# Retention and two expert blocks on one core: last Strassen product and two results of a pair moved among the next pair's, combinations on VectorE, loads two pairs ahead

## The chip, the cores and the metric

One NeuronCore of a Trainium2 chip runs the whole program. Its engines are TensorE (PE, whose weight loads are listed as PEld), VectorE (DVE), ScalarE (ACT), GpSimd (POOL) and SyncE (SP, which issues nearly all DMAs here). The metric is the device time of one execution in microseconds; lower is better.

## The reference, cut to what matters

```python
# q, k, v: (2, 8, 768, 64), lam: one decay per head
attn_out = retention(q, k, v, lam)           # decayed causal linear attention, state 64 x 64 per head
x = attn_out.transpose(0, 2, 1, 3).reshape(1536, 512)
h = x @ moe_w_in                             # 512 x 2048
x = (np.maximum(h, 0) ** 2) @ moe_w_out      # 2048 x 512
gate = 1 / (1 + np.exp(-(x @ moe2_w_gate)))  # 512 x 1536
return (gate * (x @ moe2_w_val)) @ moe2_w_out    # 1536 x 512
```

All of it is float32 on arrays of 1536 tokens. The kernel gets the weights as 64-bit numbers and turns them into float32 on the chip.

## The kernel before, in words

**Precision.** A float32 product is made from three single-pass products: each operand is split into a high half (a cast on ACT) and a low half (operand minus high half, a subtraction on DVE), and high x high, low x high and high x low are added in PSUM.

**Conversion.** The 68 weight units (128 x 512) arrive as raw 512 KB tiles, are converted by two ACT instructions (`conv_act`, L150, L151) and three DVE instructions (`conv_dve`, L172, L175, L167) and stored as 256 KB to a DRAM scratch `w32` (L169). Each `conv_act` issues the next raw load. `PACE` (L33) says how many conversions each step of phase 1 takes; `convert` (L752) places others on the agenda.

**Stages.** Tokens lie in three blocks of 512. Attention runs over 12 chunks of 128 tokens: seven ahead of the step loop, five inside it at the places of `SLOTS`. A chunk has `att_scores`, `att_prep` (on POOL `qd`, L279, and `kd`, L283; the decay mask on DVE, L289), `att_decay` (L298, POOL), `att_out` (L303: state product uv at L314, state part of the result at L323, the rest at L329), `att_state` (L336) and `att_x`. Block 0 of the tokens goes through phase 1 directly: 16 calls of `step_1`, each with 12 matmuls of `mm_in` (L393) and 12 of `mm_out` (L407). Blocks 1 and 2 together go through the input product of phase 1 by a Strassen scheme of seven block products per pair of weight units (`strassen`, L563; matmuls at L546), then through the output product (`pair_out`, L660). Phase 2 repeats this: 12 calls of `step_2`, 12 Strassen keys (gate and value for each of six pairs), `pair_out`. The last direct `stage_b` and its evacuation (`close`, L748) run inside the first Strassen pair of each phase.

**A Strassen key.** `load_a` (L506) reads two weight units as one 512 KB tile `a`. `combine_a` (L514) makes four sums and differences of its quarters into `as` on POOL (L518 to L521). `split_a` (L523) makes high halves (ACT, L527) and low halves (DVE, L528) of `a` and of `as`. The seven blocks are six matmuls each. Blocks A11, S2, S3 and A22 write bank x in that order, S1 and S4 bank z, A12 bank y. `snap` (L553, ACT) copies a bank aside; `total` (L558, DVE, L560) adds a bank and a copy. The four results go to `use`: in phase 1 a squared ReLU, in phase 2 a sigmoid (gate) or a product with the gate (value). `keep_g` (L586) stores each result (256 KB) to DRAM.

**x.** `combine_x` (L476) makes the seven x operands once per phase: differences T1 to T4 on POOL (L487), then high halves on ACT (L473) and low halves on DVE (L474).

**What sets the order.** The schedule is manual: each engine runs its instructions in the order in which the program issues them, and waits for data and for free buffers are added by the framework. A planner's clock advances by `MM` per matmul and by `SCORES` and `REST` per attention piece; `at(pos, fn)` puts work on an agenda, and `passed` runs what is due after each block of matmuls. T1 to T5 are the planned starts of the stages. Tiles come from pools of 27 tiles of 512 columns (`up`), 27 of 1024 (`wp`) and 8 PSUM banks.

```python
        block(x, key, S3, "T3", False, True)
        use(1, 1, total(x, s5), False)
        y = bank()
        block(y, key, A12, "B21", True, True)
        use(0, 0, total(y, s1), False)
        block(x, key, A22, "T4", False, True)
        use(1, 0, x, True)
```

These lines (L576 to L582) end a pair.

## Time and profile before

| what | value |
|---|---|
| median of 3 runs | 645.94 us (645.41 to 650.08) |
| the profiled execution | 650.61 us |
| its span, first to last instruction | 648.8 us |
| mean granted clock of PE, as a share of full speed | 0.968 |
| busy: PE, DVE, ACT, POOL | 604.2, 440.6, 333.1, 149.1 us |
| DMA | 127.18 MB, mean 196 GB/s |

A group is named by line, engine, operation and tiles; "idle before" is the time in which its engine had nothing running just before, and behind the arrow stands what ended that time. Matmuls are pipelined, so a group's mean exceeds the step from one matmul to the next. A stage's needs are read from that step, its losses from the waits of PE and the granted clock.

### The profile page before, as it was taken

How to read it: one execution, taken by the hardware profiler on the slowest of the kernel's cores; microseconds unless marked ns; L12 is line 12 of the kernel's file. 1: busy time of each engine (PE TensorE's matmuls, PEld its weight loads, DVE VectorE, ACT ScalarE, POOL GpSimd, SP SyncE). 2: the span in 40 equal slices, each digit the busy share in tenths (PEclk: the TensorE clock that was granted, in tenths of full speed). 3: DMA queues.
4: the chain of work that ended last, by engine and by line, in shares of the span. 5: the costliest groups of instructions: out<-in, count | busy, mean ns of one | idle time of the engine just before them, and what ended most of it. 6: DMA issues, size and time to landing. Idle time of an engine off the chain costs nothing.

```text
span 648.8 us, 8254 instructions
## 1 busy us (share of the span) xinstructions
PE 604.2 (93%) x2916; PEld 492.1 (76%) x2916; DVE 440.6 (68%) x595; ACT 333.1 (51%) x526; POOL 149.1 (23%) x122
## 2 busy tenths in 40 slices
PE   7889999995987888999999899999999999999997
PEld 6777888874765667888888688888877777778886
DVE  0799999967865566878866878776375546667201
ACT  0357788846454535756555466553544453456101
POOL 1671202129323150000003300044242345000000
PEclk9799999996988999999999799999999999999999
DMA  6967788680064437989996485540243133449003
GB/s 213 411 269 268 272 302 298 245 302 0 33 216 157 140 119 213 319 302 386 358 407 219 161 276 179 162 147 1 97 129 114 41 106 130 162 136 388 29 0 130
DMA packets 53434, 127.18 MB, mean 196 GB/s; under 512 B 5768, under 2 KB 7312, under 8 KB 53392
## 3 DMA queue, kind: packets, MB, share of 16 engines
q1 hardware_dynamic: 52376, 124.54, 54.5%
q10 hardware_dynamic: 1016, 2.11, 0.9%
q8 instruction: 23, 0.38, 0.2%
q14 instruction: 19, 0.16, 0.1%
HBM read 90.96 MB, written 35.66 MB: 195 GB/s over the span
## 4 chain that ended last, share of the span: by engine, by line
PE 72%; DVE 12%; DMA 6%; ACT 4%; issue 4%; POOL 1%; DVEq 0%; POOLq 0%; SPq 0%; ACTq 0%
PE p L660 23%; PE p L546 22%; PE p L393 14%; PE p L407 9%; DVE c L560 3%; DMA a<-w 2%; DVE al L528 2%; ACT ah L527 2%; DVE wlo L381 2%; PE p L329 1%; DMA D<-w_dram 1%; PE p L314 1%; DMA g<-g 1%; DVE m L175 1%; DVE m L172 1%
## 5 line engine op out<-in xcount | busy, mean ns | idle before, releaser
L546 PE MATMUL p<-xch,ah 128*128 128x512 f32 x280 | 113.1, 404 | 19.1 <-DVE c L560 18.4
L546 PE MATMUL p<-xcl,ah 128*128 128x512 f32 x280 | 110.8, 396 | 0.0
L546 PE MATMUL p<-xch,al 128*128 128x512 f32 x280 | 110.8, 396 | 0.0
L660 PE MATMUL p<-g2h,whi 128*128 128x512 f32 x224 | 87.1, 389 | 0.0
L660 PE MATMUL p<-g2l,whi 128*128 128x512 f32 x224 | 87.1, 389 | 0.0
L660 PE MATMUL p<-g2h,wlo 128*128 128x512 f32 x224 | 87.1, 389 | 0.0
L546 PEld LDWEIGHTS p<-xch,ah 128*128 128x128 f32 x280 | 53.6, 192 | 38.8 <-DVE c L560 26.2
L518 POOL TENSOR_TENSOR as<-a 128x512 f32<-128x512 f32 x20 | 29.1, 1457 | 205.0 <-DMA a<-w 78.8
L555 ACT COPY s<-p 128x512 f32<-128x512 f32 x60 | 35.2, 588 | 63.4 <-PE p L546 63.4
L546 PEld LDWEIGHTS p<-xch,al 128*128 128x128 f32 x280 | 53.5, 191 | 11.5
L546 PEld LDWEIGHTS p<-xcl,ah 128*128 128x128 f32 x280 | 53.6, 192 | 10.6
L528 DVE TENSOR_TENSOR al<-a,ah 128x1024 fp32r<-128x1024 f32 x20 | 27.7, 1384 | 46.3 <-ACT ah L527 44.7
L381 DVE TENSOR_TENSOR wlo<-u,whi 128x512 fp32r<-128x512 f32 x68 | 54.6, 831 | 2.2 <-ACT whi L379 0.8
L167 DVE CUSTOM_DVE_ANT_0 u<-m,r 128x1024 uint16<-128x1024 uint16 x68 | 53.5, 787 | 3.6 <-PE p L660 0.5
L175 DVE SCALAR_TENSOR_TENSOR m<-j,m 128x512 int32<-128x512 int32 x68 | 51.9, 763 | 1.3
L393 PE MATMUL p<-xh,wlo 128*128 128x512 f32 x160 | 44.8, 403 | 6.5 <-DVE wlo L381 6.5
L150 ACT ACTIVATE j<-raw 128x512 f32<-128x512 f32 x68 | 45.6, 671 | 8.6 <-PE p L407 3.4
L660 PEld LDWEIGHTS p<-g2l,whi 128*128 128x128 f32 x224 | 42.0, 188 | 8.8
L660 PEld LDWEIGHTS p<-g2h,whi 128*128 128x128 f32 x224 | 42.0, 188 | 8.7
L660 PEld LDWEIGHTS p<-g2h,wlo 128*128 128x128 f32 x224 | 42.0, 188 | 8.7
L151 ACT ACTIVATE r<-raw 128x512 int32<-128x512 uint32 x68 | 45.1, 663 | 6.4 <-PE p L660 4.9
L379 ACT CAST whi<-u 128x512 fp32r<-128x512 f32 x68 | 38.8, 617 | 14.7 <-DVE u L167 11.2
(86 smaller groups left out, 1045.9 us busy)
## 6 DMA issues: line engine op xcount, KB each, us to landing
raw<-in_w SPq DMA_DIRECT2D x68, 512.0 KB, 5.7
w<-u SPq DMA_DIRECT2D x68, 256.0 KB, 3.7
u<-w SPq DMA_DIRECT2D x64, 256.0 KB, 5.0
g<-g SPq DMA_DIRECT2D x56, 256.0 KB, 3.1
g<-g SPq DMA_DIRECT2D x28, 512.0 KB, 6.8
a<-w SPq DMA_DIRECT2D x20, 512.0 KB, 5.1
kv<-in_kv SPq DMA_DIRECT2D x12, 512.0 KB, 9.5
qk<-in_qk SPq DMA_DIRECT2D x10, 512.0 KB, 4.8
```

The source lines that it names most:

```text
L150: nc.scalar.activation(j, t[:, :, 1].bitcast(F32), AF.Copy, scale=2.0**-112)
L151: nc.scalar.activation(r, t[:, :, 0].bitcast(mybir.dt.uint32), AF.Copy, scale=2.0**-29)
L167: nc.vector.tensor_tensor(out=w.bitcast(I32), in0=m, in1=r, op=ALU.add)
L175: lambda: nc.vector.scalar_tensor_tensor(out=m, in0=j, scalar=-(2**31), in1=m, op0=ALU.bitwise_and, op1=ALU.bitwise_or),
L379: nc.scalar.copy(hi, src)
L381: lambda lo=lo, src=src, hi=hi: nc.vector.tensor_tensor(out=lo, in0=src, in1=hi, op=ALU.subtract)
L393: nc.tensor.matmul(acc, lhsT=a[:, kk * P : (kk + 1) * P], rhs=b[:, kk, :], start=i == 0, stop=i == 11,)
L407: nc.tensor.matmul(acc[e], lhsT=a[:, e * P : (e + 1) * P], rhs=b, start=first and i == 0, stop=last and i == 2,)
L528: nc.vector.tensor_tensor(out=lo, in0=src, in1=hi, op=ALU.subtract)
L546: nc.tensor.matmul(acc, lhsT=w[:, col, kk * P : (kk + 1) * P], rhs=x[:, kk, :], start=start and i == 0, stop=stop and i == 5, skip_group_c ...
L555: nc.scalar.copy(s, acc)
L660: nc.tensor.matmul(acc[e, t], lhsT=a[:, e * P : (e + 1) * P], rhs=b[:, t, :], start=first and i == 0, stop=last and i == 2,)
```

## The change

Within `strassen`, now one loop over all keys of a phase, block A22 and the results of A12 and A22 of a pair are issued inside the next pair: the sum for A12's result behind the next pair's A11 matmuls, A22 and its result behind the snap of the next pair's A11. `combine_a` and the differences of `combine_x` are issued on DVE instead of POOL. A key's load is issued at the start of the pair two ahead; high halves, combination and low halves for the next pair stand at fixed places in the pair. Results of a pair are stored together in the next pair. No conversions are placed in phase 1's products; 24 instead of 20 are placed in its output stage. PACE falls from 3 to 2 in steps 6 and 11, and to 1 and 0 in steps 14 and 15; as a step converts only while more than 36 units are left (`step_1`), step 13, which took none before, then takes two. Stores of converted weights fall due 4.0 instead of 1.0 planned us after conversion. In attention, uv and the state part are computed per head on tiles of 64, the state holds only the diagonal 64 x 64 blocks, `kd` is issued ahead of `qd`, and the state part comes after the rest. The weights of phase 2's first steps are loaded and split earlier. Agenda places and the planner's constants change accordingly.

```diff
-PACE = (2, 2, 2, 2, 2, 2, 3, 2, 2, 2, 2, 3, 2, 2, 2, 2)
+PACE = (2, 2, 2, 2, 2, 2, 2, 2, 2, 2, 2, 2, 2, 2, 1, 0)
...
-SCORES = 1.1
-REST = 3.3
+SCORES = 1.2
+REST = 2.6
...
-            at(clock[0] + 1.0, lambda: nc.sync.dma_start(out=w32[ph][f, u], in_=w))
+            at(clock[0] + 4.0, lambda: nc.sync.dma_start(out=w32[ph][f, u], in_=w))
...
-    S = [const.tile([P, 4, P], F32, name=f"S{i}", tag=f"S{i}") for i in range(2)]
+    S = [const.tile([P, 4, 64], F32, name=f"S{i}", tag=f"S{i}") for i in range(2)]
...
-        for st in S:
-            nc.vector.memset(st, 0.0)
...
-        if n > 0:
-            qd = qd_t[c] = unit("qd")
-            nc.gpsimd.tensor_tensor(out=pv(qd), in0=pv(qt), in1=L, op=ALU.mult)
...
+        if n > 0:
+            qd = qd_t[c] = unit("qd")
+            nc.gpsimd.tensor_tensor(out=pv(qd), in0=pv(qt), in1=L, op=ALU.mult)
...
-                out=pv(tt), in0=S[c // SEQ_CH],
-                in1=L[:, :, CH - 1 : CH].to_broadcast([P, 4, P]), op=ALU.mult,
+                out=pv(tt)[:, :, 0:64], in0=S[c // SEQ_CH],
+                in1=L[:, :, CH - 1 : CH].to_broadcast([P, 4, 64]), op=ALU.mult,
...
+        heads = [(p, r, slice(64 * r, 64 * r + 64)) for p in range(4) for r in range(2)]
...
         if n < SEQ_CH - 1:
-            kd = kd_t.pop(c)
-            uv = pv(bank())
-            for p in range(4):
+            kd = kd_t.pop(c).rearrange("s (h d) -> s h d", h=H)
+            uv = bank()[:, 0:256].rearrange("a (p e) -> a p e", p=4)
+            for p, r, b in heads:
                 nc.tensor.matmul(
-                    uv[:, p, :], lhsT=pv(kd)[:, p, :], rhs=pv(vt)[:, p, :], start=True, stop=True
+                    uv[b, p, :], lhsT=kd[:, 2 * p + r, :], rhs=v[:, 2 * p + r, :],
+                    start=p == 0, stop=p == 3, skip_group_check=True,
                 )
...
+        for p, r, b in heads:
+            nc.tensor.matmul(
+                ov[b, p, :], lhsT=v[:, 2 * p + r, :], rhs=pv(at[:, r, :])[:, p, :],
+                start=p == 0, stop=n == 0 and p == 3, skip_group_check=True,
+            )
...
-            qd = qd_t.pop(c)
...
+            qd = pv(qd_t.pop(c))
+            for p, r, b in heads:
                 nc.tensor.matmul(
-                    ov[:, p, :], lhsT=s[:, p, :], rhs=pv(qd)[:, p, :], start=p == 0, stop=False,
-                    skip_group_check=True,
-                )
...
-                    start=n == 0 and p == 0, stop=p == 3, skip_group_check=True,
+                    ov[b, p, :], lhsT=s[b, p, :], rhs=qd[b, p, :],
+                    start=False, stop=p == 3, skip_group_check=True,
...
-        ops = []
-        for r in range(2 if uv is not None else 0):
-            b = slice(64 * r, 64 * r + 64)
-            if tt is None:
-                ops.append(lambda b=b: nc.scalar.copy(s[b, :, b], uv[b, :, b]))
-            else:
-                ops.append(
-                    lambda b=b: nc.vector.tensor_tensor(
-                        out=s[b, :, b], in0=uv[b, :, b], in1=pv(tt)[b, :, b], op=ALU.add
-                    )
-                )
-        return ops
+        if uv is None:
+            return []
+        if tt is None:
+            return [lambda: nc.scalar.copy(s, uv)]
+        return [
+            lambda: nc.vector.tensor_tensor(out=s, in0=uv, in1=pv(tt)[:, :, 0:64], op=ALU.add)
+        ]
...
         nc.scalar.copy(hi, src)
-        nc.vector.tensor_tensor(out=lo, in0=src, in1=hi, op=ALU.subtract)
-
-    def combine_x(early, pos, gap):
-
+        at(
+            clock[0] + 1.3,
+            lambda: nc.vector.tensor_tensor(out=lo, in0=src, in1=hi, op=ALU.subtract),
+        )
...
-        at(early, lambda: split_x("B11", b11))
-        at(early + gap, lambda: split_x("B21", b21))
...
-            nc.gpsimd.tensor_tensor(
-                out=t[name], in0=t.get(a, a) if isinstance(a, str) else a,
-                in1=t[b] if isinstance(b, str) else b, op=ALU.subtract,
+            nc.vector.tensor_tensor(
+                out=t[name], in0=a, in1=t[b] if isinstance(b, str) else b, op=ALU.subtract
             )
...
             lambda: diff("T1", b12, b11),
             lambda: split_x("T1", t["T1"]),
             lambda: diff("T2", b22, "T1"),
             lambda: split_x("T2", t["T2"]),
+            lambda: split_x("B22", b22),
             lambda: diff("T3", b22, b12),
-            lambda: split_x("B22", b22),
             lambda: split_x("T3", t["T3"]),
             lambda: diff("T4", b21, "T2"),
             lambda: split_x("T4", t["T4"]),
...
-        tt = nc.gpsimd.tensor_tensor
+        tt = nc.vector.tensor_tensor
...
-    def split_a(key, part):
-        src = (a_t, as_t)[part].pop(key)
+    def high_a(key, part):
         hi = wp.tile([P, 4, 256], F32R, tag="w", name="ah")
         lo = wp.tile([P, 4, 256], F32R, tag="w", name="al")
-        nc.scalar.copy(hi, src)
+        nc.scalar.copy(hi, (a_t, as_t)[part][key])
+        s_t[(*key, part)] = hi, lo
+
+    def low_a(key, part):
+        hi, lo = s_t[(*key, part)]
+        src = (a_t, as_t)[part].pop(key)
         nc.vector.tensor_tensor(out=lo, in0=src, in1=hi, op=ALU.subtract)
-        s_t[(*key, part)] = hi, lo
 
     def prepare_a(key, pos):
 
-        at(pos - 22.0, lambda: load_a(key))
-        at(pos - 15.0, lambda: combine_a(key))
-        at(pos - 8.0, lambda: split_a(key, 0))
-        at(pos - 5.0, lambda: split_a(key, 1))
+        at(pos - 24.0, lambda: load_a(key))
+        at(pos - 14.0, lambda: combine_a(key))
+        at(pos - 12.0, lambda: high_a(key, 0))
+        at(pos - 9.0, lambda: low_a(key, 0))
+        at(pos - 8.0, lambda: high_a(key, 1))
+        at(pos - 5.0, lambda: low_a(key, 1))
...
-    def strassen(key, use, between=None):
...
+    def strassen(keys, uses, between):
+
+
+
+        after = between
+        for n, (key, use) in enumerate(zip(keys, uses, strict=True)):
+            nxt = keys[n + 1] if n + 1 < len(keys) else None
+            if n + 2 < len(keys):
+                load_a(keys[n + 2])
+            stores, held[:] = list(held), []
+            x = bank()
+            block(x, key, A11, "B11", True, True)
+            if n:
+                after[0]()
+            if nxt:
+                high_a(nxt, 0)
+                combine_a(nxt)
+            s1 = snap(x)
+            after[1]()
+            if nxt:
+                high_a(nxt, 1)
+            z = bank()
+            block(z, key, S1, "T1", True, True)
+            s5 = snap(z)
+            if nxt:
+                low_a(nxt, 0)
+            block(x, key, S2, "T2", False, True)
+            s2 = snap(x)
+            if nxt:
+                low_a(nxt, 1)
+            for fn in stores:
+                fn()
+            block(z, key, S4, "B22", False, True)
+            use(0, 1, total(z, s2), False)
+            block(x, key, S3, "T3", False, True)
+            use(1, 1, total(x, s5), False)
+            y = bank()
+            block(y, key, A12, "B21", True, True)
+
+            def first(use=use, y=y, s1=s1):
+                use(0, 0, total(y, s1), False)
+
+            def second(use=use, x=x, key=key):
+                block(x, key, A22, "T4", False, True)
+                use(1, 0, x, True)
+                for part in range(2):
+                    s_t.pop((*key, part))
+
+            after = first, second
+        after[0]()
+        after[1]()
+        for fn in held:
+            fn()
+        held.clear()
...
     def keep_g(ph, f, t, g):
-        at(clock[0] + 1.0, lambda: nc.sync.dma_start(out=g_dram[ph][f, :, t], in_=g))
-
-    def pair_in_1(i, between=None):
+        held.append(lambda: nc.sync.dma_start(out=g_dram[ph][f, :, t], in_=g))
...
-        combine_x(T1 - 40.0, T1 - 15.0, 1.6)
+        keys = [(1, i, 0) for i in range(NF1 // 2)]
+        prepare_a(keys[0], T1)
+        at(T1 - 20.0, lambda: load_a((1, 1, 0)))
+        combine_x([T1 + d for d in (-30, -25, -15, -13, -11, -9, -7, -4, -2, 1, 3)])
         for f in range(NF1):
             step_1(f)
-        n_in, n_out = 4, 20
-        for k in range(n_in):
-            convert(T1 + 10.0 + k * (T2 - T1 - 14.0) / n_in)
+        n_out = 24
...
+        uses = [use for i in range(NF1 // 2) for use in pair_in_1(i)]
+        strassen(keys, uses, (None, lambda: close(1)))
...
         for f in range(2):
-            at(T3 - 20.0 + f, lambda f=f: load_units(2, f))
-        at(T3 - 8.0, lambda: run(split_w(2, 0)))
...
-        for k in range(3 * NF2 - n_in - n_out):
+        for k in range(3 * NF2 - n_out):
...
+        keys = [(2, i, u) for i in range(NF2 // 2) for u in range(2)]
+        prepare_a(keys[0], T4)
+        at(T4 - 20.0, lambda: load_a((2, 0, 1)))
+        combine_x([T4 - 46.0 + 3.5 * k for k in range(11)])
```

## Rows read from the trace of the kernel before

**Rows 1.** The page, first part: busy us and share of the span.
```profile
PE 604.2 (93%) x2916; PEld 492.1 (76%) x2916; DVE 440.6 (68%) x595; ACT 333.1 (51%) x526; POOL 149.1 (23%) x122
```

**Rows 2.** Windows by stage: us; busy PE, PEld, DVE, ACT, POOL; clock; DMA; GB/s.
```profile
0.00:45.40 45.40, 36.88 (x364) 33.16 (x364) 25.98 (x44) 13.55 (x24) 23.46 (x23) 0.89 0.84 313
45.40:143.40 98.00, 96.39 (x559) 78.45 (x558) 93.54 (x149) 75.17 (x130) 17.51 (x12) 1.00 0.79 279
143.40:165.80 22.40, 13.96 (x42) 10.31 (x40) 16.52 (x10) 13.10 (x18) 19.40 (x12) 0.70 0.03 13
165.80:266.20 100.40, 85.74 (x350) 67.67 (x349) 64.66 (x82) 48.96 (x76) 26.24 (x24) 0.95 0.49 163
266.20:353.40 87.20, 87.20 (x386) 72.26 (x385) 66.55 (x98) 50.48 (x79) 1.89 (x1) 1.00 0.94 342
353.40:454.70 101.30, 98.17 (x421) 80.65 (x421) 80.13 (x103) 54.24 (x89) 23.50 (x16) 0.97 0.46 152
454.70:579.80 125.10, 120.61 (x517) 95.92 (x517) 69.36 (x85) 61.05 (x90) 37.13 (x36) 1.00 0.33 110
579.80:645.10 65.30, 65.26 (x288) 53.68 (x287) 23.16 (x28) 16.54 (x22) 0.00 (x0) 1.00 0.38 139
```

**Rows 3.** Waits of PE: who was waited for, us in total, times, longest.
```profile
PE p L546 <- DVE c L560: 18.4, 14, 3.8
PE p L407 <- ACT gh L434: 6.7, 1, 6.7
PE p L393 <- DVE wlo L381: 6.5, 4, 3.1
```

**Rows 4.** Window inside PE's longest wait in the step loop.
```profile
147.00:151.00 4.00, 0.00 (x0) 0.00 (x0) 1.72 (x1) 2.73 (x5) 3.92 (x3) 0.50 0.00 0
```

**Rows 5.** Timelines near 143 us: start, us, instruction, [idle before].
```profile
142.53 1.29 POOL L518 TENSOR_TENSOR as<-a 128x512 f32<-128x512 f32 x1 [16.83 <-DMA a<-w]
...
148.21 1.04 ACT L473 CAST xch<-t 128x1024 fp32r<-128x1024 f32 x1 [10.29 <-POOL t L487]
```

**Rows 6.** Timelines of DVE and POOL: the low half alone, and beside POOL.
```profile
213.06 1.23 DVE L528 TENSOR_TENSOR al<-a,ah 128x1024 fp32r<-128x1024 f32 x1 [2.80 <-ACT ah L527]
...
229.28 1.56 DVE L528 TENSOR_TENSOR al<-as,ah 128x1024 fp32r<-128x1024 f32 x1
...
229.72 1.70 POOL L521 TENSOR_TENSOR as<-a,as 128x256 f32<-128x256 f32 x1
```

**Rows 7.** Timelines of POOL and DVE at the start of phase 2's step loop.
```profile
354.23 2.46 POOL L487 TENSOR_TENSOR t<-xr,t 128x1024 f32<-128x1024 f32 x1 [0.31 <-POOL t L487]
...
354.47 2.77 DVE L175 SCALAR_TENSOR_TENSOR m<-j,m 128x512 int32<-128x512 int32 x1
```

**Rows 8.** Groups by line over the whole span: shape, count, busy us, mean ns.
```profile
L560 DVE TENSOR_TENSOR c<-p,s 128x512 f32<-128x512 f32 x60 | 39.6, 681 | 0.6 <-PE p L546 0.4
...
L555 ACT COPY s<-p 128x512 f32<-128x512 f32 x60 | 35.2, 588 | 63.4 <-PE p L546 63.4
...
L527 ACT CAST ah<-a 128x1024 fp32r<-128x1024 f32 x20 | 21.0, 1050 | 0.0
```

**Rows 9.** DMA issues of product weights; SP's longest wait.
```profile
a<-w SPq DMA_DIRECT2D x20, 512.0 KB, 5.1
...
SPq L509 <- DVE xcl L474: 25.0, 1, 25.0
```

**Rows 10.** Timeline of PE: the three matmul groups of one chunk's results.
```profile
113.31 1.05 PE L314 MATMUL p<-kv,kd 128*128 128x128 f32 x8
114.20 1.06 PE L323 MATMUL p<-qd,S 128*128 128x128 f32 x8
115.19 1.09 PE L329 MATMUL p<-at,kv 128*64 128x128 f32 x16
```

**Rows 11.** Windows of 10 us, output stage of phase 1.
```profile
270.00:280.00 10.00, 10.00 (x46) 8.26 (x45) 7.92 (x12) 5.45 (x9) 0.00 (x0) 1.00 1.01 348
...
330.00:340.00 10.00, 10.00 (x46) 8.29 (x45) 6.39 (x10) 5.14 (x8) 0.00 (x0) 1.00 1.04 408
```

More of the change, by code (lines that the diff above doesn't have):

```diff
@@ L336, in att_state @@
     def att_state(c):
-        n = c % SEQ_CH
         s = S[c // SEQ_CH]
@@ L502, in combine_x @@
         ]
-        for k, fn in enumerate(todo):
-            at(pos + k * gap, fn)
+        for pos, fn in zip(places, todo, strict=True):
+            at(pos, fn)
     def load_a(key):
@@ L561, in total @@
         return c
-    def strassen(key, use, between=None):
-        x, z = bank(), bank()
-        block(x, key, A11, "B11", True, True)
-        s1 = snap(x)
-        block(z, key, S1, "T1", True, True)
-        s5 = snap(z)
-        if between:
-            between()
-        block(x, key, S2, "T2", False, True)
-        s2 = snap(x)
-        block(z, key, S4, "B22", False, True)
-        use(0, 1, total(z, s2), False)
-        block(x, key, S3, "T3", False, True)
-        use(1, 1, total(x, s5), False)
-        y = bank()
-        block(y, key, A12, "B21", True, True)
-        use(0, 0, total(y, s1), False)
-        block(x, key, A22, "T4", False, True)
-        use(1, 0, x, True)
-        for part in range(2):
-            s_t.pop((*key, part))
+    def strassen(keys, uses, between):
[46 more added lines that the diff above has]
+        held.clear()
@@ L606, in use, with pair_in_2 @@
             keep_g(1, 2 * i + di, t, g)
-        strassen((1, i, 0), use, between)
-    def pair_in_2(i, between=None):
+        return [use]
+    def pair_in_2(i):
         gate = {}
@@ L805, in retention_moe_kernel @@
             prepare_out(1, f, T2 + 24 * MM * f)
-        for i in range(NF1 // 2):
-            pair_in_1(i, lambda: close(1) if i == 0 else None)
+        uses = [use for i in range(NF1 // 2) for use in pair_in_1(i)]
+        strassen(keys, uses, (None, lambda: close(1)))
         xc.clear()
@@ L827, in retention_moe_kernel @@
             prepare_out(2, f, T5 + 24 * MM * f)
-        for i in range(NF2 // 2):
-            pair_in_2(i, lambda: close(2) if i == 0 else None)
+        uses = [use for i in range(NF2 // 2) for use in pair_in_2(i)]
+        strassen(keys, uses, (None, lambda: close(2)))
         pair_out(2)
```

27 lines of the change are left out of this document (10 added, 17 removed).

## Prediction, before the change was run

> **What bounds the kernel now.** I read the page's first part, then the windows by stage, the waits of PE, the timelines around the long waits, and the groups by line.
>
> TensorE (PE) is busy for 93% of the span [rows 1]; the question is where the missing time lies. A 512-column matmul is issued every 0.2267 us where nothing waits: the output stage of phase 1 runs 384 of them in 87.05 us, and the windows put that stage at 87.2 us with PE always busy [rows 2]. Counting matmuls by that step gives what each stage would need (my stretches):
>
> - first steps up to 143.4 us: 98.0 us, PE idle 1.6;
> - end of the step loop, 143.4 to 165.8: 40 matmuls, 9.1 us; took 22.4: 13.3 lost;
> - Strassen products of phase 1: 8 keys of 42 plus 12, 78.9 us; took 100.4: 21.5 lost;
> - step loop of phase 2: 420, 95.2 us; took 101.3: 6.1 lost;
> - Strassen products of phase 2: 12 keys of 42 plus 12, 117.0 us; took 125.1: 8.1 lost;
> - both output stages: nothing lost.
>
> So 49 us are lost after the start, and they are waits, plus the slower clock that follows them. [rows 3] gives the kinds: 18.4 us of PE in 14 waits on `total` (L560), one of 6.7 us on a cast of ScalarE (ACT), 6.5 us on low halves of weights. After the wait of 6.7 us PE stood at a granted clock of 0.50 [rows 4], the lower of its two levels (1.2 of 2.4 GHz); the stage's mean was 0.70, that of phase 1's products 0.95 [rows 2], which alone is 5.0 of its 21.5 us.
>
> Causes. (a) In a pair the last block (A22) adds to bank x and must wait for the `total` that reads x; only block A12 (six matmuls, 1.36 us) lies between, and VectorE (DVE) does low halves and squares ahead of that `total`. (b) At 143 us GpSimd (POOL) starts the weight combination only when its load has landed, then does the x differences; ACT sits 10.3 us on the first of them, in front of the activations that PE needs [rows 5]. (c) Beside POOL, DVE's instructions on SBUF stretch: the same low half took 1.23 us alone and 1.56 beside POOL [rows 6]; at phase 2's start one instruction of a conversion took 2.77 us while POOL ran a difference [rows 7] that nobody needed for 50 us, and PE then waited 3.1 us for a low half [rows 3].
>
> **The change, part by part.** Sums are made against the profiled execution: 648.8 us of span and 1.8 around it, 650.6. That is 4.7 above the median of the runs, 645.9; I build the new time from counted work, take nothing off for it and let the lower end hold it.
>
> *Pipeline over pairs.* A22 of pair n-1 now comes after A11 of pair n, so two blocks (2.72 us) lie between S3 and A22. Is that enough? DVE's list per pair, by [rows 8]: three totals at 0.68, three squares at the same, two low halves at 1.23 [rows 6], and the combination, new on DVE: one of 512 columns (0.68) and three of 256. Those three are not in the trace on DVE; between half of 0.68 and 0.68 each, I take 0.42, nearest to half with a fixed part, 1.9 in all (1.7 to 2.7). Sum 8.4 us (8.2 to 9.2) of a pair's 9.52. DVE fits, in this order (0 is the start of A11): total and square 0.2 to 1.5, combination to 3.4, square of A22's result to 4.2, low halves to 6.6, total and square of z 7.0 to 8.3, total of x to 9.05. A22 is due at 10.88: 1.8 us of slack. ACT has two high halves at 1.05 and three snaps at 0.59 [rows 8] and in phase 1 three activations of a snap's width, 5.6 us. Its tight place is the snap of z: behind the second high half, which waits for the combination (3.5 to 4.5), it ends at 5.1, and S4 needs it at 5.44: 0.3 us. In phase 2 the value keys carry four products instead of three squares, 9.1 us: still under 9.52. So steady pairs should run without waits.
>
> The first pair carries more: the 12 matmuls of `close`, four casts and subtractions of `evacuate`, the last x terms; DVE some 12.6 us against 12.2. I leave 2.0 us lost in phase 1 (bounds 0, and 10 if half the present waits stay) and 0.8 in phase 2 (0 to 4). Gains: 21.5 - 2.0 = 19.5, and 8.1 - 0.8 = 7.3.
>
> *Loads two pairs ahead, stores grouped.* A load comes 9.5 us before its pair's turn and 11.0 before DVE wants it; they land in a median of 5.1 us [rows 9]. The load, then four grouped stores, share SP's queue; the stores' producers are done half a pair earlier, so SP waits for none. Cost nothing; uncovered, it is rival 4. The converted weights' stores, due 4.0 instead of 1.0 later, move no bytes. Buffers are tight: 14 x halves, 3 raw weights and the pairs' tiles make 27 of 27 when the combination is written, by my count; a wait for a free one would be on work already done.
>
> *Combinations on DVE at the end of the step loop.* Off goes wait (b), 13.3 us with its clock. In its place DVE gets, in the last 16.3 us, three x differences at 1.23 (a 1024-column instruction alone), the combination 1.9, five low halves 6.2, the steps' own four splits and three low halves 4.8, and two conversions that PACE moves here, at most three instructions of 0.68 each, 4.1: 20.7. That is over the room by 4.4 us; starts overlap, so I leave 3.0 lost (0.5 to 10). DVE is queued in order, so weight halves behind a difference are what PE would wait for. Gain 10.3.
>
> *Attention.* uv becomes 16 instructions of 64 moving columns for 8 of 128; the state part 16 of 64 rows for 8. Today these take 0.89 and 0.99 us from start to start, the 16 column-tiled ones of the third group 1.02 [rows 10]. uv: half of 1.02 at best, 1.02 at worst, I take 0.65, nearer to half as the columns halve; state part 0.5 to 1.02, I take 0.95, near today's 0.99. In the loop three chunks have the first and five the second: 3 x 0.24 + 5 x 0.04 = 0.9 us (-0.6 to +3.6). One state addition instead of two and half a decay on POOL also shorten the DVE and POOL queues; with `kd` ahead of `qd` the waits on L314 and the first low halves shrink: I estimate 2.0 us (0 to 4) over the seven chunks of the first 45.4 us, half an addition's 0.68 [rows 8] each, and 0.8 of the 1.6 idle in the loop. Gain 3.7.
>
> The Trainium skill, "TensorEngine Tiling (Array Packing)", section Instruction Overhead, speaks against the first of these: some 60 cycles are paid per matmul whatever its columns, and a small dimension should not be tiled again. By it uv would stay at the 1.02 us of its 16 instructions and this part would lose about 1 us; no row before shows 64 columns.
>
> *Output stage of phase 1.* Four conversions (768 KB each with the store: 3.15 MB in all) leave the products and come here, 24 for 20. The stage moved 342 GB/s at a DMA share of 0.94 [rows 2]: 29.8 MB; now 33.0. While the queues were full they moved 348 to 408 GB/s (the upper in [rows 11]), mean of six such stretches of 10 us, the first and last of which stand there, 378: 87.3 us for a stage of 87.05. Casts are placed 6.5 us ahead, and two casts and two low halves take some 3.5 [rows 6, 8], so a load may be 3 us late unseen. I take 1.0 us lost (0, as margin and unevenly used stretches absorb it, to 8.3, the extra bytes at 378).
>
> The Trainium skill, "SBUF — State Buffer", section Summary: rules for kernel authors, counts on about 358 GB/s between HBM and SBUF; 33.0 MB would then take 92.2 us, an estimate, 5 over the stage. [rows 11] shows 408 over 10 us, so I keep that for a rival.
>
> *Start of phase 2.* The weights' loads go 4 us and the first split 6 us earlier, and POOL's differences move to DVE 46 us before the products, after the conversions' stretch. DVE has 21 us free of 101.3 [rows 2]; four differences are 4.9. I leave 0.6 of 6.1 (0 to 3). Gain 5.5.
>
> Sum of gains: 19.5 + 7.3 + 10.3 + 3.7 - 1.0 + 5.5 = 45.3; 650.6 - 45.3 = **605.3 us**.
>
> **The rivals.**
> 1. *Output stage bound by DMA*: 8.3 instead of 1.0, 612.6 us. For: queues full at a share of 1.04 [rows 11]. Against: the stores no longer hold up SP, stretches at the stage's ends are free. By the figure that the Trainium skill gives above, 5 would stand for the 8.3.
> 2. *The end of the loop only changes its engine*: ACT's wait for POOL becomes PE's wait for DVE, 10 of 13.3 lost again: 612.3. For: DVE was busy 93.5 of 98 us there [rows 2].
> 3. *The pipeline does half of what it says*: `total` stays late behind combination and low halves: 10 and 4 lost in the products, +11.2: 616.5. For: 88% of DVE. Against: the slack of 1.8 us.
> 4. *Slower: a late load stops DVE.* The combination stands in DVE's queue behind the last `total` and before all that A22 needs. A load landing x us after its place delays A22 by x - 12.8 (11.0 and the slack), at 16 keys that are loaded so. Break-even with the gain of 45.3 is x = 15.6; at 16.5 it costs 59: 664 us. For: one load waited 25.0 us for a buffer in SP's queue [rows 9]. Against: median 5.1, and buffers are freed earlier now.
> 5. *Every cover holds*, and attention gains its upper bound: about 595.
>
> **How the numbers follow.** Forecast 0.58; rival 1 0.15, 2 0.10, 3 0.09, 4 0.04, 5 0.04. The forecast's own range is 600 to 610. To hold 8 in 10 I go from 597 (most covers) to 621 (rival 3 with some of another). About 1% is what a measurement of this kernel tells from no change: 639.5 and below is faster. Rivals 1 to 3, even two at once, stay below that, so faster 0.94, same 0.02 (several together), slower 0.04.
>
> **What would show it.** Right: no wait of PE on L560 over 1 us; granted clock 1.00 in both product stages; POOL empty after the last chunk; product stages near 81 and 118 us; the loop's end near 12; phase 2's loop near 96. Wrong steps: PE waits on weight low halves around 140 us (rival 2), gaps in the output stage with ACT waiting on DMA (rival 1), DVE waiting on `a<-w` (rival 4), the snap of z ending after S4's turn. The forecast is wrong if the product stages together lose over 12 us, or the time is outside 597 to 621.

## The result and the profile after

The changed kernel took 602.68 us (median of four runs, 601.90 to 603.98) where the kernel before took 646.45 (645.41 to 650.08): a ratio of 0.9316, interval 0.9275 to 0.9356. The forecast was 605.3 us in a range of 597 to 621. The profiled executions went from 650.61 to 602.85 us, their spans from 648.8 to 600.8.

The windows by stage of the changed kernel, in the columns of [rows 2], cut at the same places of the program (first steps, end of the step loop, products, output stage, and so on):

```profile
0.00:41.50 41.50, 32.61 (x460) 28.64 (x460) 23.40 (x39) 12.86 (x22) 21.73 (x23) 0.92 0.91 343
41.50:137.30 95.80, 95.36 (x622) 76.26 (x621) 90.36 (x148) 78.27 (x135) 14.74 (x11) 1.00 0.80 283
137.30:147.30 10.00, 9.34 (x41) 7.42 (x40) 9.96 (x14) 6.14 (x9) 0.00 (x0) 1.00 0.29 103
147.30:231.60 84.30, 80.67 (x349) 64.80 (x349) 68.58 (x100) 47.26 (x73) 0.00 (x0) 1.00 0.44 150
231.60:318.70 87.10, 87.10 (x386) 72.13 (x385) 73.63 (x110) 55.42 (x87) 0.00 (x0) 1.00 0.94 365
318.70:413.90 95.20, 95.20 (x422) 78.85 (x421) 74.81 (x112) 55.29 (x91) 0.00 (x0) 1.00 0.52 174
413.90:531.10 117.20, 117.20 (x517) 96.76 (x516) 85.15 (x129) 60.14 (x89) 0.00 (x0) 1.00 0.35 117
531.10:595.90 64.80, 64.80 (x287) 53.67 (x287) 23.11 (x27) 15.95 (x21) 0.00 (x0) 1.00 0.36 137
```

From 231.6 us on TensorE's busy time equals the length of every window, and the granted clock is 1.00 in all stages behind the first. The end of the step loop, 22.4 us at a clock of 0.70 before, takes 10.0 at 1.00. Most of what is still lost lies in the first 41.5 us and in one stage: the products of phase 1 take 84.3 us for 78.9 of work.

The waits of PE in the changed kernel, which answer to [rows 3]:

```profile
PE p L314 <- POOL kd L278: 3.6, 3, 1.9
PE p L264 <- DMA qk<-in_qk: 2.6, 2, 1.6
PE p L400 <- ACT gh L427: 2.4, 1, 2.4
...
PE p L386 <- DVE wlo L374: 1.0, 2, 0.7
...
PE p L545 <- DVE c L559: 0.6, 1, 0.6
PE p L545 <- ACT s L554: 0.6, 2, 0.3
```

The 18.4 us on `total` (now L559) have become 0.6, the 6.5 on low halves 1.0, the 6.7 on a cast 2.4. That last wait is the largest part of the 5.4 us that the products of phase 1 still lose. A timeline of the changed kernel around it, three engines in turn (start, us, instruction, idle before):

```profile
148.40 1.05 ACT L466 CAST xch<-t 128x1024 fp32r<-128x1024 f32 x1 [4.23 <-DVE t L480]
149.36 0.59 ACT L417 ACTIVATE r<-p 128x512 f32<-128x512 f32 x1
...
150.64 0.62 ACT L427 CAST gh<-g 128x512 fp32r<-128x512 f32 x1
...
147.15 1.22 DVE L480 TENSOR_TENSOR t<-xr 128x1024 f32<-128x1024 f32 x1
...
151.31 0.50 PE L400 MATMUL p<-gh,whi 128*128 128x512 f32 x1 [2.44 <-ACT gh L427]
```

It is the pattern of [rows 5] in small: ScalarE sits 4.23 us on the cast of a difference (T3) that VectorE starts only at 147.15, and the last activation of the step loop, which TensorE wants at once, stands behind it in ScalarE's queue.

### The profile page after: what moved, and what is told of

Read it like the earlier page. It is cut to its first block, busy times and chain, and to the rows that moved or that the text cites. A ratio compares the mean times of both kernels' runs of the same rounds, so it can differ in the third digit from the quotient of the medians.

```text
span 600.8 us, 8489 instructions
## 1 busy us (share of the span) xinstructions
PE 583.0 (97%) x3076; PEld 478.8 (80%) x3076; DVE 449.8 (75%) x673; ACT 331.9 (55%) x524; POOL 36.5 (6%) x34
## 4 chain that ended last, share of the span: by engine, by line
PE 84%; DVE 9%; DMA 3%; ACT 2%; issue 2%; POOL 0%; DVEq 0%; ACTq 0%; SPq 0%; POOLq 0%
PE p L545 30%; PE p L692 25%; PE p L386 16%; PE p L400 10%; DVE xcl L469 1%; PE p L322 1%; DMA D<-w_dram 1%; DVE m L175 1%; DVE wlo L374 1%; DVE u L167 1%; PE p L329 1%; DVE t L480 1%; PE p L264 1%; DMA lam_sb<-in_lam 1%; DVE at L287 1%
## 5 line engine op out<-in xcount | busy, mean ns | idle before, releaser
L545 PE MATMUL p<-xch,ah 128*128 128x512 f32 x280 | 109.6, 391 | 1.2 <-DVE c L559 0.6
L545 PE MATMUL p<-xcl,ah 128*128 128x512 f32 x280 | 109.0, 389 | 0.0
L545 PE MATMUL p<-xch,al 128*128 128x512 f32 x280 | 109.0, 389 | 0.0
L692 PE MATMUL p<-g2h,whi 128*128 128x512 f32 x224 | 87.1, 389 | 0.0
L692 PE MATMUL p<-g2l,whi 128*128 128x512 f32 x224 | 87.1, 389 | 0.0
L692 PE MATMUL p<-g2h,wlo 128*128 128x512 f32 x224 | 87.1, 389 | 0.0
L559 DVE TENSOR_TENSOR c<-p,s 128x512 f32<-128x512 f32 x60 | 41.2, 688 | 26.6 <-PE p L545 22.1
L545 PEld LDWEIGHTS p<-xcl,ah 128*128 128x128 f32 x280 | 52.6, 188 | 10.7
L167 DVE CUSTOM_DVE_ANT_0 u<-m,r 128x1024 uint16<-128x1024 uint16 x68 | 50.0, 736 | 2.7
L374 DVE TENSOR_TENSOR wlo<-u,whi 128x512 fp32r<-128x512 f32 x68 | 46.2, 708 | 7.0 <-ACT whi L372 5.7
L175 DVE SCALAR_TENSOR_TENSOR m<-j,m 128x512 int32<-128x512 int32 x68 | 49.5, 728 | 1.2
L372 ACT CAST whi<-u 128x512 fp32r<-128x512 f32 x68 | 39.1, 618 | 13.8 <-DVE u L167 13.3
L386 PE MATMUL p<-xh,wlo 128*128 128x512 f32 x160 | 43.2, 392 | 1.1 <-DVE wlo L374 1.0
L386 PE MATMUL p<-xh,whi 128*128 128x512 f32 x160 | 43.8, 395 | 0.0
```

Of the source, the lines that this page charges most:

```text
L167: nc.vector.tensor_tensor(out=w.bitcast(I32), in0=m, in1=r, op=ALU.add)
L175: lambda: nc.vector.scalar_tensor_tensor(out=m, in0=j, scalar=-(2**31), in1=m, op0=ALU.bitwise_and, op1=ALU.bitwise_or),
L372: nc.scalar.copy(hi, src)
L374: lambda lo=lo, src=src, hi=hi: nc.vector.tensor_tensor(out=lo, in0=src, in1=hi, op=ALU.subtract)
L386: nc.tensor.matmul(acc, lhsT=a[:, kk * P : (kk + 1) * P], rhs=b[:, kk, :], start=i == 0, stop=i == 11,)
L545: nc.tensor.matmul(acc, lhsT=w[:, col, kk * P : (kk + 1) * P], rhs=x[:, kk, :], start=start and i == 0, stop=stop and i == 5, skip_group_c ...
```

## The experiments

All twelve kernels compute everything. The first stage has the same code in ten kernels (the changed one and nine experiments made from it), and took 40.2 to 45.0 us there. In the three that took 44.6 to 45.0 (e1, e4, e10) the DMA queues moved 297 to 315 GB/s from 10 to 20 us and the granted clock from 20 to 30 us was 0.63 to 0.65; in the other seven it was 324 to 345 GB/s and 0.94 to 1.00. What starts this is not shown. So one execution can differ from another by up to 5 us for reasons that are no part of an edit, and I read the edits from the stages behind it. Each ratio is against the kernel before as it ran beside that experiment (medians 645.79 to 648.34 us). Stage lengths in us run from the first matmul of a stage to the first of the next, in the profiled execution:

| kernel | median us | ratio, interval | loop 1 | products 1 | output 1 | loop 2 | products 2 |
|---|---|---|---|---|---|---|---|
| before | 646.45 | | 120.4 | 100.4 | 87.2 | 101.3 | 125.1 |
| changed | 602.68 | 0.9316 [0.9275, 0.9356] | 105.8 | 84.3 | 87.1 | 95.2 | 117.2 |
| e1_own_pair | 612.01 | 0.9445 [0.9394, 0.9495] | 105.6 | 91.1 | 87.1 | 95.2 | 118.4 |
| e2_pool_a | 607.55 | 0.9391 [0.9331, 0.9450] | 108.1 | 86.4 | 87.1 | 95.7 | 117.2 |
| e3_pool_x | 606.37 | 0.9357 [0.9312, 0.9402] | 112.9 | 79.4 | 87.1 | 97.2 | 117.3 |
| e4_conv_in | 606.19 | 0.9364 [0.9315, 0.9414] | 105.7 | 88.3 | 87.0 | 95.2 | 117.2 |
| e5_before_dve | 632.89 | 0.9767 [0.9738, 0.9796] | 111.4 | 99.6 | 87.1 | 95.2 | 124.7 |
| e6_before_places | 630.63 | 0.9738 [0.9708, 0.9769] | 121.6 | 88.5 | 87.0 | 100.3 | 117.3 |
| e7_late_half | 602.80 | 0.9307 [0.9281, 0.9333] | 106.2 | 83.9 | 87.1 | 95.2 | 117.3 |
| e8_late_own | 617.60 | 0.9537 [0.9510, 0.9564] | 105.8 | 91.7 | 87.0 | 95.2 | 124.6 |
| e9_t3_late | 600.71 | 0.9290 [0.9259, 0.9320] | 105.8 | 81.3 | 87.0 | 95.2 | 117.3 |
| e10_conv30 | 608.09 | 0.9410 [0.9373, 0.9446] | 105.4 | 84.3 | 92.5 | 95.2 | 117.3 |
| e11_load_late | 601.46 | 0.9311 [0.9275, 0.9348] | 105.9 | 83.9 | 87.1 | 95.2 | 117.3 |
| e12_dve_places | 615.42 | 0.9530 [0.9486, 0.9575] | 112.6 | 89.0 | 87.0 | 95.2 | 117.6 |

### The pipeline over pairs

**Undone in the changed kernel.** The results of A12 and A22, and the block A22, go back to the end of their own pair.

```diff
-            if n:
-                after[0]()
...
-            after[1]()
+            if n == 0:
+                between[1]()
...
-            after = first, second
-        after[0]()
-        after[1]()
+            first()
+            second()
```

> The changed kernel, with block A22 and the results of A12 and A22 issued again at the end of their own pair; everything else as changed (combinations on VectorE, loads two ahead, no conversions in the products). Theory A, the place of A22 is what removed the waits on `total`: one block of 1.36 us lies again between S3 and A22, so PE waits for L559 in most of the 20 pairs, some 0.5 to 1.0 us each with the restart, 10 to 18 us in all: 613 to 621 us. Theory B, the waits came from what stood ahead of `total` in VectorE's queue (stretched low halves, conversions), and those are gone: by the order worked out for a pair, the total of x ends 0.4 us before A22 is due even at the old place, so the time stays within 3 us: 602 to 606 us.

612.01 us, between the two theories. The products of phase 1 lose 6.8 us more than in the changed kernel, those of phase 2 only 1.2, where the kernel before lost 8.1. The waits of PE in this kernel; its timeline in a steady pair of phase 1 (ACT, PE) and in a value key of phase 2 (DVE):

```profile
PE p L545 <- ACT s L554: 2.8, 6, 0.5
...
PE p L545 <- DVE c L559: 1.9, 1, 1.9
```

```profile
183.46 1.05 ACT L520 CAST ah<-as 128x1024 fp32r<-128x1024 f32 x1 [0.94 <-DVE as L515]
184.42 1.06 ACT L554 COPY s<-p 128x512 f32<-128x512 f32 x2
...
185.05 0.50 PE L545 MATMUL p<-xch,ah 128*128 128x512 f32 x1 [0.50 <-ACT s L554]
...
458.70 1.22 DVE L526 TENSOR_TENSOR al<-as,ah 128x1024 fp32r<-128x1024 f32 x1 [0.21 <-ACT ah L520]
461.21 0.69 DVE L559 TENSOR_TENSOR c<-p,s 128x512 f32<-128x512 f32 x1 [1.28 <-PE p L545]
```

Without the pipeline TensorE of phase 1 waits for a snap in every steady pair: the combination comes late on VectorE, behind the totals of the pair before, ScalarE waits 0.94 us for it, and the snap of z stands behind. That is the place that the prediction called tight (0.3 us of room). The rest of the 6.8 us comes mostly from the one wait of 1.9 us on `total`, in the first pair, and from the clock behind it, by this window of e1:

```profile
167.20:171.20 4.00, 3.97 (x10) 3.20 (x11) 1.66 (x3) 2.29 (x4) 0.00 (x0) 0.57 0.51 197
```

In the value key nothing on TensorE waits for `total`: VectorE has the second low half done and is idle 1.28 us before the next total. So something else had removed the wait on `total` in phase 2. In `split_a`'s agenda the second low half came behind block S4; the change also moved it ahead, right behind the first.

**The second low half back behind S4, with the pipeline (e7) and without it (e8).**

```diff
-            if nxt:
-                high_a(nxt, 1)
...
-            if nxt:
-                low_a(nxt, 1)
...
             block(z, key, S4, "B22", False, True)
+            if nxt:
+                high_a(nxt, 1)
+                low_a(nxt, 1)
```

> The changed kernel, with the second high and low half of the next pair put directly ahead of the total of z, where they stood before; A22 stays in the next pair. Theory C with two covers: the total of x then ends about 10.5 us after the start of the pair's A11; A22 is due at 10.9, so it still fits: phase 2's products stay within 2 us of 117.3, phase 1's within 4 of 84.3, 602 to 608 us. If the place of the halves alone decides, products lose 0.7 to 1 us per key: 616 to 623 us.

> Both undone in the changed kernel: second halves directly ahead of the total of z, and A22 with the two results in their own pair. Theory C with two covers: neither undone alone costs much in phase 2, both together do; the total of x ends about 10.5 us after the start of A11 and A22 is due at 9.5: about 1 us and the restart per key, phase 2's products 127 to 132 us, phase 1's 95 to 100: 625 to 640 us. Theory B, the totals were only late because of GpSimd and conversions, which are gone here: as with A22 alone in its own pair, 610 to 615 us.

e8 is this edit and e1's together. e7 is the changed kernel within 0.2 us; e8 takes 617.60 us, less than the 625 to 640 of its theory C, and has most of phase 2's loss back, 124.6 us. Its waits of PE, and its timeline in a value key (ACT, DVE, PE):

```profile
PE p L545 <- DVE c L559: 10.0, 12, 1.7
```

```profile
458.31 1.05 ACT L520 CAST ah<-as 128x1024 fp32r<-128x1024 f32 x1
...
459.39 1.23 DVE L526 TENSOR_TENSOR al<-as,ah 128x1024 fp32r<-128x1024 f32 x1 [2.93 <-ACT ah L520]
460.53 0.68 DVE L559 TENSOR_TENSOR c<-p,s 128x512 f32<-128x512 f32 x1
461.25 0.69 DVE L648 TENSOR_TENSOR g<-c,r 128x512 f32<-128x512 f32 x1
461.86 0.68 DVE L559 TENSOR_TENSOR c<-p,s 128x512 f32<-128x512 f32 x1
...
462.60 0.50 PE L545 MATMUL p<-xch,ah 128*128 128x512 f32 x1 [0.79 <-DVE c L559]
```

VectorE idles 2.93 us for a high half whose cast is issued late, behind the snap of S2 on ScalarE, then does the low half in front of two totals and a product, and A22 is 0.79 us late. Each of the two edits is enough in phase 2 (e1 loses 1.2 us there, e7 0.1); only without both does the loss come back.

**The places alone, in the kernel before.**

```diff
-        at(pos - 8.0, lambda: split_a(key, 0))
-        at(pos - 5.0, lambda: split_a(key, 1))
+        at(pos - 9.0, lambda: split_a(key, 0))
+        at(pos - 7.0, lambda: split_a(key, 1))
```

> The kernel before, with one thing changed: the two splits of the next pair's weights stand at 9 and 7 planned us ahead instead of 8 and 5, which puts the second high and low half behind block S1 instead of behind S4. Theory C, the products lost time because the second low half, waiting for its high half on ScalarE, stood in VectorE's queue directly ahead of the totals: phase 2's products go from 125.1 to 117 to 120 us, phase 1's (with conversions and GpSimd as before) from 100.4 to 86 to 95: 627 to 637 us. Theory A, it is the place of A22, one block behind S3: products within 3 us of before, 642 to 648 us.

Two numbers in the kernel before, and it takes 630.63 us, as theory C had it: the products of phase 2 go to 117.3, those of phase 1 from 100.4 to 88.5. The wait on `total` of 18.4 us in 14 [rows 3] is now, among PE's waits,

```profile
PE p L546 <- DVE c L560: 4.9, 3, 2.2
```

### The combinations on VectorE

**Weight combinations back on POOL (e2), x differences back on POOL (e3)**, each in the changed kernel:

```diff
     def combine_a(key):
...
-        tt = nc.vector.tensor_tensor
+        tt = nc.gpsimd.tensor_tensor
```

> The changed kernel with the weight combination (four instructions per key) on GpSimd again; the pipeline and everything else stay. Theory A, the engine matters by its speed and by what it does to VectorE beside it: the four take about 4.5 us there instead of 1.9, the second high half and with it the snap of z come 2 to 3 us late, low halves stretch from 1.23 to 1.5 us and more: PE waits on L554 about 1.5 to 2.5 us per pair, 25 to 45 us in all: 628 to 648 us. Theory B, the pipeline alone hides the combination wherever it runs: within 4 us of the changed kernel, 602 to 607 us.

```diff
         def diff(name, a, b):
...
-            nc.vector.tensor_tensor(
+            nc.gpsimd.tensor_tensor(
```

> The changed kernel with the differences T1 to T4 of x on GpSimd again. Theory A, they caused the loss at the end of the step loop and at the start of phase 2: ScalarE sits again on the first difference, VectorE is stretched beside GpSimd; 5 to 12 us come back at the end of the loop. In phase 2 they now stand late on the agenda, but GpSimd is free and starts when the data are there, so 2 to 5 us come back at its start: 609 to 619 us. Theory B, the late load of the first combination caused it (it is issued two planned us earlier now): at most 3 us come back, 602 to 606 us.

e2: 607.55 us, near theory B. 2.3 us more in the loop, 2.1 in the products of phase 1, nothing in phase 2's products. Steady pairs don't lose by the engine that combines, though low halves beside POOL take up to 1.88 us in e2; the first combination does. PE's wait on `gh` grows:

```profile
PE p L400 <- ACT gh L427: 5.1, 2, 4.3
```

e3: 606.37 us, between the two theories. The loop takes 7.1 us more, phase 2's loop 2.0, the products of phase 1 4.9 less, as the differences run early on POOL and leave VectorE free by then. The price is a late low half of weights in the loop:

```profile
PE p L386 <- DVE wlo L374: 7.5, 4, 5.7
```

It is late because VectorE's weight combination now runs beside the differences on POOL. One instruction of each in e3, and the same VectorE instruction in the changed kernel:

```profile
131.86 2.74 POOL L480 TENSOR_TENSOR t<-xr,t 128x1024 f32<-128x1024 f32 x1
132.25 2.63 DVE L513 TENSOR_TENSOR as<-a 128x256 f32<-128x256 f32 x1
```

```profile
132.51 0.42 DVE L513 TENSOR_TENSOR as<-a 128x256 f32<-128x256 f32 x1
```

The four instructions of that combination take 2.91, 2.63, 2.59 and 2.56 us, 10.7 in all instead of 1.9; the low half stands behind them. ScalarE waits only 0.4 us for a difference in this stretch, so what comes back in e3 is not wait (b) of the prediction but the stretching of (c).

**Both on VectorE, in the kernel before (e5), and that with e6's two numbers (e12).** e5 is e2's and e3's line in the other direction; e12 is e5 and e6 together.

> The kernel before, with the weight combinations and the x differences on VectorE, at the places where it had them; no pipeline, conversions stay in the products. Theory A, GpSimd cost the most at the end of the step loop and at the start of phase 2: these two stages get shorter by about 8 and 5 us. In the products the combination then stands in VectorE's queue ahead of the totals of its pair (15 planned us before the next pair): 0 to 1 us more per key, 0 to 20 us. In all 633 to 650 us. Theory B, the engine is the main cause in the products too: all stages shorten, 620 to 630 us.

> The kernel before with two small edits together, each tried alone already (x differences and weight combinations on VectorE: ratio 0.977; the second low half directly behind the first in ScalarE's and VectorE's order: 0.974). If they act on different waits, as the stages say (the end of the loop and phase 2's loop by the one, the products by the other), they add: ratio 0.945 to 0.955, 611 to 617 us, with phase 2's products at 117 to 118 us, its loop at 95 to 96, and the first loop near 111. Rival (the vector engine with both becomes the bound of the products, and the pipeline over pairs is what makes room for the combination there): products of phase 1 stay near 99 and the ratio near 0.97.

e5: 632.89 us. The loop is 9.0 us shorter, phase 2's loop 6.1 and at its 95.2 us of work; the products keep their losses. Its wait on `total`:

```profile
PE p L546 <- DVE c L560: 16.9, 12, 3.8
```

e12: 615.42 us, where the sum of the two single gains (15.1 and 16.9 us against a kernel before of about 646) gives 614. The two act on different waits and add. Windows of e12 for the products of phase 1 and of phase 2, in the columns of [rows 2]:

```profile
155.50:244.50 89.00, 82.28 (x350) 64.16 (x349) 73.19 (x110) 50.70 (x80) 0.00 (x0) 1.00 0.54 178
...
426.70:544.30 117.60, 117.60 (x517) 96.50 (x516) 83.34 (x125) 60.68 (x90) 0.00 (x0) 1.00 0.35 117
```

So some 30 of the 44 us come from an engine's name in two places and two numbers in an agenda; the rest of the change, the pipeline, the attention and the placing of conversions among it, brings the other 13.

### Conversions and the output stage

**Four conversions back among the products (e4); six more in the output stage (e10).**

```diff
-        n_out = 24
+        n_in, n_out = 4, 20
+        for k in range(n_in):
+            convert(T1 + 10.0 + k * (T2 - T1 - 14.0) / n_in)
...
```

> The changed kernel with four conversions placed in phase 1's products again and 20 in the output stage. If VectorE's spare 1.1 us per pair is the limit (theory A), each conversion of about 2 us makes the total of x and the snaps late in its pair: 1 to 2 us each, 4 to 8 us in all, 606 to 611 us. If the 1.8 us of slack at A22 takes them up (theory B), at most 2 us: 602 to 605 us. The output stage loses nothing in the changed kernel, so nothing comes back there.

```diff
-        n_out = 24
+        n_out = 30
```

> The changed kernel with 30 weight conversions instead of 24 in the output stage of phase 1, and six fewer after it: 4.7 MB more in a stage that moved 365 GB/s x 87.1 us = 31.8 MB. It asks how far the stage of 87.05 us was from a bound by DMA. With the forecast's 378 GB/s for full queues, 36.5 MB take 96.6 us: 9.5 us slower. With the 397 to 415 GB/s that the changed kernel showed in its full stretches they take 88 to 92 us: 1 to 5 us slower. If DMA is no limit at all, 0. The step loop of phase 2, which lost nothing, has nothing to give back.

e4: the products lose 4.0 us more, and the output stage gains nothing. PE waits for snaps, which stand behind the conversions' activations on ScalarE:

```profile
PE p L545 <- ACT s L554: 2.9, 6, 0.9
```

e10: the output stage takes 92.5 us, 5.4 more; by the mean rate of its window (393 GB/s over 92.5 us) it moved 36.4 MB. Windows of e10 in that stage, whole and near its end, and ScalarE's longest wait there:

```profile
234.30:326.80 92.50, 89.19 (x385) 73.11 (x384) 83.04 (x128) 61.85 (x98) 0.00 (x0) 0.98 1.00 393
...
314.00:324.00 10.00, 6.69 (x23) 4.78 (x22) 9.29 (x15) 7.44 (x13) 0.00 (x0) 0.84 1.04 416
```

```profile
ACT j L150 <- DMA raw<-in_w: 14.0, 11, 2.4
```

Here the stage is bound by DMA: the share is over 1 from 244 us to the end, and ScalarE waits for raw weights eleven times. The same windows of the changed kernel, which [rows 11] answers to, show the queues just as full, but emptied before the stage ends:

```profile
241.60:251.60 10.00, 10.00 (x46) 8.29 (x45) 9.62 (x15) 7.27 (x12) 0.00 (x0) 1.00 1.02 397
...
261.60:271.60 10.00, 10.00 (x46) 8.29 (x45) 9.09 (x14) 6.81 (x11) 0.00 (x0) 1.00 1.04 415
...
301.60:311.60 10.00, 10.00 (x45) 8.29 (x45) 6.52 (x10) 7.77 (x13) 0.00 (x0) 1.00 0.77 308
```

### Loads one pair ahead

```diff
-            if n + 2 < len(keys):
-                load_a(keys[n + 2])
+            if n and nxt:
+                load_a(nxt)
```

> The changed kernel with each pair's raw weights loaded one pair ahead instead of two, for the 16 keys that are loaded inside the pipeline. If a load starts when its pair does (the order of the program, as rival 4 of the prediction counted), it has 1.4 us of cover for a landing of 4.2 us (median); the combination and then A22 would be 1 to 3 us late at 16 keys: 16 to 48 us slower. If SyncE's queue runs ahead of TensorE and is held only by stores and by buffers, as the issue times in the trace of the changed kernel suggest (13.8 us from the issue of a load to its combination, not 11.0), the load still has some 9.5 us and the time stays within 2 us.

601.46 us, no later than the changed kernel. The issue of the last load of phase 1's products and the combination that needs it, in the timelines of the changed kernel and then of e11:

```profile
198.69 0.37 SPq L503 DMA_DIRECT2D a<-w  x1
...
212.50 0.68 DVE L512 TENSOR_TENSOR as<-a 128x512 f32<-128x512 f32 x1
```

```profile
205.89 0.37 SPq L503 DMA_DIRECT2D a<-w  x1
...
211.49 0.68 DVE L512 TENSOR_TENSOR as<-a 128x512 f32<-128x512 f32 x1
```

One pair ahead in the program still leaves 5.6 us in the steady pairs of phase 1 (4.2 in one pair, 9.6 and more in those of phase 2), and a load took 4.0 us (median of e11). SyncE is ahead of TensorE: in e11 it waits 61.4 us for engines to be done with what stands in the buffers of the loads (L503) and 64.3 for results to store (L620). The second pair of lead is cover that this kernel doesn't use.

### The first pair

**T3's cast behind the last activation.** One number of the changed kernel's `combine_x` call:

```diff
-        combine_x([T1 + d for d in (-30, -25, -15, -13, -11, -9, -7, -4, -2, 1, 3)])
+        combine_x([T1 + d for d in (-30, -25, -15, -13, -11, -9, -7, -4, 0.5, 1, 3)])
```

> The changed kernel with one number altered: the cast of the x difference T3 is put at +0.5 instead of -2 (in us around the start of the products), so the last activation of the step loop stands ahead of it on ScalarE. Theory (ScalarE, queued in order, sat 4.23 us on that cast while the activation behind it was what TensorE's wait of 2.44 us in the first pair wanted): the products of phase 1 take 80 to 82 us instead of 84.3, the kernel 599 to 601 us. Rival (VectorE is late in that stretch whatever ScalarE's order is): the wait moves to a low half or a total, the stage stays within 1 us of 84.3 and the time within 1 us of the changed kernel's.

The products of phase 1 take 81.3 us, 3.0 less, and the wait on `gh` is gone. ScalarE's timeline in e9:

```profile
145.87 0.62 ACT L427 CAST gh<-g 128x512 fp32r<-128x512 f32 x1
148.15 1.05 ACT L466 CAST xch<-t 128x1024 fp32r<-128x1024 f32 x1 [1.66 <-DVE t L480]
```

Counted from the start of the stage, the cast that TensorE wanted ends 4.5 us earlier, and the wait for VectorE falls behind it, where nobody needs ScalarE. The median, 600.71 us, is the lowest of all kernels here, but its interval overlaps that of the changed kernel: the 3 us are shown by the stage, not by the totals. 2.4 us of the stage stay lost, half of it in two waits for snaps (1.2 us).

## Why the prediction was right

Gains in us between the two profiled executions, by the stretches that the prediction cut:

| term | predicted | measured |
|---|---|---|
| products of phase 1 | 19.5 | 100.4 - 84.3 = 16.1 |
| products of phase 2 | 7.3 | 125.1 - 117.2 = 7.9 |
| end of the step loop | 10.3 | 22.4 - 10.0 = 12.4 |
| attention, first stage and loop | 3.7 | 3.9 + 2.2 = 6.1 |
| output stage of phase 1 | -1.0 | 0.1 |
| start of phase 2 | 5.5 | 6.1 |
| sum | 45.3 | 48.7 |

The spans differ by 48.0: from the first matmul of the last stage to the end the changed kernel takes 0.4 us more, and the rest is rounding. On the medians the gain is 43.8. The forecast built 605.3 from counted work against an execution of 650.61 that lay 4.2 above the median, and the changed kernel's was 602.85; the sum was 3.4 us short, and no term was off by more than that. Part of this closeness is luck: the products of phase 1 gave 3.4 us less than their term, the other five together 6.8 more.

**Products.** That the wait for `total` goes once two blocks lie between was right in effect and incomplete as a cause. The prediction's cause (a) named both halves, only one block between and low halves ahead of the total, but credited the pipeline alone. In phase 2 either edit is enough (e1, e7), and only e8, with neither, loses 7.6 of the 8.1 us again. In phase 1, taking the pipeline out of the changed kernel costs 6.8 us (e1): 3.1 at waits for snaps, counted from matmul to matmul less the step of 0.2267 us, and most of the rest in one wait for `total` and the lower clock behind it. Not all of this need belong to the pipeline: e12 has none either, has four conversions among these products, and takes 89.0 us, 2.1 less than e1.

**The first pair**, 2.0 us, was the mis-sized term: 5.4 were lost. VectorE was late there, as the prediction had it, but the prediction left out that the cast of a late difference would stand in front of a wanted activation on ScalarE: 3.0 us by e9. With e9's order the stage loses 2.4, near the 2.0.

**End of the loop.** 0.9 us lost instead of 3.0. VectorE was as full as the prediction counted (9.96 us busy of 10.0), but the price shows in the first pair: with the differences off VectorE its stage loses only 0.5 (e3). So the two mis-sized terms look like one debt, paid a stage later; that reading is argued. Moving only the x differences back costs the loop 7.1 us, by stretching (e3), and only the weight combination 2.3 (e2); in the kernel before, moving both to VectorE gives 9.0 (e5). The other 5.6 of the loop's 14.6 us (attention, conversions at other steps, an earlier load) were not tried one by one. The prediction gave the clock of 0.50 in [rows 4] as the one after the wait; that row lies inside it, and from 151 to 155 us, behind it, the clock was 0.50 too.

**Beside POOL.** Cause (c) held, and was larger than the prediction's 1.56 for 1.23 us let expect (e3's combination, 10.7 for 1.9). The low half of `as`, which took up to 1.83 us in the kernel before, never takes more than 1.23 after the change; and phase 2's loop comes to its 95.2 us by the move off POOL alone (e5), and leaves it when the differences alone move back (e3, 97.2).

**Attention.** The group of uv, in a timeline of PE in the changed kernel, with the two that follow it, answers to [rows 10]:

```profile
107.51 0.69 PE L314 MATMUL p<-kv,kd 128*64 128x64 f32 x16
108.02 1.04 PE L322 MATMUL p<-at,kv 128*64 128x128 f32 x16
109.00 1.09 PE L329 MATMUL p<-qd,S 64*64 64x128 f32 x16
```

From start to start uv takes 0.51 us, the lower bound (half of 1.02) and not the 0.65 taken. That is 32 ns each, where the 16 instructions of 128 columns behind it take 61. The state part, from 109.00 to 110.02 us, took its upper bound of 1.02. The prediction was wrong to read a time of 1.02 us for uv out of the Trainium skill, "TensorEngine Tiling (Array Packing)", section Instruction Overhead: it says that a matmul of one column takes as long as one of 60, and 64 columns lie above that. The trace does not speak against it, and no run here has fewer columns. The first stage gained 3.9 us instead of 2.0, but it moves by as much between executions of one code, and its granted clock from 20 to 30 us was 0.81 before and 0.98 after, so neither number can be called confirmed.

**Rivals.** Rival 1 (output stage bound by DMA) did not come, and e10 shows how near it was: four conversions more than before were free, ten cost 5.4 us. Its price came from a mean of 378 GB/s over stretches with a DMA share of 0.99 to 1.04, which moved 348 to 408; at 1.02 to 1.04 the changed kernel moved 397 to 415, and the whole stage 31.8 MB (365 GB/s over 87.1 us), not the 33.0 counted. The Trainium skill's 358 GB/s ("SBUF — State Buffer", section Summary: rules for kernel authors) is passed by 39 to 57 GB/s in these stretches of the changed kernel. Rival 2 came only as the loss in the first pair, 3.0 us by e9 and 4.9 by e3. Rival 3 fell: `total` costs 0.6 us in all. Rival 4's mechanism was not met at all: its lead of 11.0 us was 13.8 in the steady pairs of phase 1, and even 5.6 was enough (e11). A load later than that was not tried.

## What to carry to other kernels

Where a wait names an engine, ask first what stands ahead of the wanted instruction in that engine's queue and whether it could be issued earlier or later: here two numbers in an agenda (e6) bought 17 us, one more (e9) 3 us of a stage, and both looked like a busy engine in the profile. Work on a second engine was no gain here where it sat in front of, or ran beside, the work that TensorE waits for: the differences moved onto the busiest side engine and the loop became shorter. And undo the parts of a change in pairs, not only one by one: e1 and e7 alone would each have said that its edit does next to nothing for phase 2.

## What the runs showed of the hardware that was not expected

- 16 matmuls of 64 moving columns, on two column tiles in turn, took 0.51 us, 32 ns each; the same number with 128 columns took 0.98.
- The DMA queues moved 412 to 417 GB/s in windows of 10 us for as long as they were kept full (e10, from 254 to 324 us).
- With no instruction on POOL, VectorE's 1024-column subtractions take 1.21 to 1.23 us in all of the 40 low halves of weights; with POOL running beside them, in the kernel before, the same ones took up to 1.83.
- A VectorE subtraction of 256 columns took 2.56 to 2.63 us beside a POOL difference (e3, three of them) and 0.42 with POOL idle (the changed kernel). Each of the three ended 0.28 us after the POOL instruction that it ran beside.
